# An attention and gated feed-forward kernel: the output stage's first product ordered behind the middle stage's last, the last group's chunks in another order, and their results through four buffers

## The chip, the core and the metric

The kernel runs on one core of a Trainium2 chip. The metric is the device time of one execution in microseconds (us), as the median of several runs. A profile of one execution gives the rows quoted below. TensorE (PE) does the matrix products, VectorE (DVE), ScalarE (ACT) and GpSimd (POOL) the element-wise work, and SyncE (SP) issues the transfers (DMA), one after another in a fixed order.

## What is computed

```python
# q, k, v: batch 8, heads 8, sequence 576, head size 64
scores = scale * q @ k.T + alibi_bias            # causal, window of 128
attn = softmax(scores)                           # with 1e-9 in the denominator
x = (attn @ v) as 4608 tokens x 512
gate = 1 / (1 + exp(-(x @ w_gate)))              # 512 x 1536
val = x @ w_val                                  # 512 x 1536
out = (gate * val) @ w_out                       # 1536 x 512
```

## The kernel before

All operations are first collected in a list, `Graph`. Each has an engine, a guessed cost, the keys that it reads and writes, and a wish time. `Graph.order` then plans one fixed order for every engine by these guesses, and the instructions are written in that order. At run time each engine goes through its own list in order and waits for semaphores where it depends on others. So an operation that waits holds everything behind it on its engine, and a changed key or guessed cost can move any operation.

The work has three stages. In the first, attention for 8 batches of 4 head pairs goes along with a first part of the feed-forward products (L528). The middle stage (`ffn2`, products in L662) makes gate and value for six groups of tokens, t = 0 to 5, of 768 tokens each, in halves of 384. The output stage (`last`, products in L780) multiplies the result by w_out, group after group, and writes the output.

Middle and output stage use a scheme with seven products where a plain 2 by 2 block product takes eight. An operand is first combined (sums and differences of its four blocks), then each combination is split into a high and a low part, and a product is six matmuls: two blocks times high-high, high-low and low-high. In the middle stage a chunk is one slice of 128 of the 1536 hidden columns: seven products over the combinations xc0 to xc6 (buffers ar0 to ar6), accumulated in three of the eight PSUM banks. `chunk` writes them in the order 0, 3, 4, 1, 5, 2, 6. Between them ScalarE copies partial results out (`low`, and p5 in `later_hs`), VectorE adds them to the next ones (L669), ScalarE takes a tanh (`sg`, L673) and VectorE multiplies (L677). The result of a chunk, 128 by 2 by 384, stays in a buffer `later_hs`, of which there are two, taken in turn, until a DMA has stored it in the scratch tensor `hid`.

The chunk's weights lie in one of eight slots, `w2s0` to `w2s7`, high and low part apart (w2s60 and w2s61 are slot 6). The middle stage runs groups 4 and 5 first and group 3 last. In group 3 eight chunks are left, on slots 0 to 7. When a slot's last chunk is done, the slot is filled again for the output stage: slots 0 to 5 with w_out (`wo20` to `wo25`, from the scratch `stash_o`), slots 6 and 7 with part of the hidden results of a group (`rows60` to `rows71`, from `hid`). The rest of these rows goes to `rows_xr`, where the middle stage's input was. Which rows lie where is said by

```python
    RAW = {(0, 0, 0): 0, (0, 0, 1): 1, (0, 0, 2): 2, (1, 0, 0): 3, (1, 1, 0): 4, (1, 0, 1): 5, (1, 1, 1): 6, (1, 0, 2): 7,
           (1, 1, 2): 8, (0, 1, 0): 9, (0, 1, 1): 10, (0, 1, 2): 11}
```

for (half, block, part q): places 0 to 3 are in `rows_xr`, 4 to 7 in slot 6, 8 to 11 in slot 7. The output stage goes through its combinations k in the order 0, 3, 4, 1, 5, 2, 6, each for three parts q and two output blocks j. k = 0 uses a row as it is, k = 3 a sum of two (`csum`), k = 4 this sum less a third. A combination's high and low part is a `duo`, in the buffers ar7, 0, 3, 4, 1, 5, 2, 6 in turn; all but the first are those of xc, so a duo can be written when the last middle product of that xc is done. k = 0, parts 0 to 2, are duo7, duo0 and duo3; k = 3 are duo4, duo1 and duo5; k = 4 begins with duo2 and duo6. The sum csum0 needs slot 6's rows, csum2 slot 7's.

Other buffers around the meeting of the stages: `wtmp`, two tiles in which w_out is prepared before it is stored in `stash_o`, on the tags h3 and h4; later on `csmall` and `cout0` lie there. `follow` hands a place from one set of keys to the next without an instruction.

Of the kernel before, what the change touches and what calls it, by code (L numbers as in the profile page):

```python
# [163 lines left out]
def attention_gated_ffn(ctx: ExitStack, tc: tile.TileContext, qd, kd, vd, wg, wv, wo, out):  # L164
# [334 lines left out]
    def hs(e, name="later_hs"):  # L499
        return T(moe, f"{name}{e}", [P, 2, N2] if name == "later_hs" else [P, NB], F32, tag=f"hs{e}")  # L500

# [106 lines left out]

    def ffn2(t, w, todo, F):
        made = t in held  # L610
# [39 lines left out]
        def chunk(i, fc):  # L650
            bx, by, bz = bank(), bank(), bank()
            e = turns[0] % 2
            turns[0] += 1
# [4 lines left out]
            def product(k, b, start, wk):  # L658
                def six():
                    for c in range(2):  # L660
                        for j, (xp, wp) in enumerate(((0, 0), (0, 1), (1, 0))):
                            nc.tensor.matmul(mm[b][:, 0:N2], w.tile2(i, wp)[:, wk, c * P:(c + 1) * P], combo(k, xp)[:, c],  # L662
                                             start=(start and c == 0 and j == 0), stop=(c == 1 and j == 2), skip_group_check=True)
                wa = 0 if wk < 2 else 2
                g.add("PE", 6 * (N2 / 2400 + 0.0133), six, [("ar", k, 0), ("ar", k, 1), ("w2", i, 0, wa), ("w2", i, 1, wa)],
                      [("mm", b)], 1.0e6)
# [31 lines left out]
            c, q, m = place(fc)  # L698
            move(lambda: hid[c, q, t][m].rearrange("p (h t) -> p h t", h=2), lambda: hs(e), [kp, kv], [("hid", fc, t, 0)], F, N2)

# [20 lines left out]
    def last(t):  # L721
        F = FIRST + 2
        n = 2 * N2
        for q in range(NDUO):
            for h, c in ((0, 0), (1, 0), (1, 1), (0, 1)):
                reads = [k for m in range(2) for k in g.writer if k[0] == "hid" and k[1] == 4 * q + 2 * m + c and k[2] == t]
                move(lambda h=h, c=c, q=q: raw2(h, c, q),
                     lambda h=h, c=c, q=q: hid[c, q, t][:, :, h * N2:(h + 1) * N2].rearrange("m p t -> p m t"),
                     reads, [("raw", h, c, q)], F + 0.1 * (h + c), n / 2)
        x = {(h, c, q): (lambda h=h, c=c, q=q: raw2(h, c, q)) for h, c, q in RAW}  # L730
# [22 lines left out]
        for k in ORDER:  # L753
# [19 lines left out]
            for j in range(2):  # L773
                bx, by, bz = bks[j]
                b = {0: bx, 3: bz, 4: bx, 1: by, 5: bx, 2: bz, 6: bx}[k]
                for q, (r, duo) in enumerate(ring):
                    def six(q=q, duo=duo, b=b, j=j, k=k):
                        for m in range(2):
                            for e, (xp, wp) in enumerate(((0, 0), (0, 1), (1, 0))):
                                nc.tensor.matmul(mm[b][:, 0:N2], wo2(2 * q + m, wp)[:, k, j * P:(j + 1) * P], duo(xp)[:, m],  # L780
                                                 start=(k in (0, 3, 1) and q == 0 and m == 0 and e == 0),
                                                 stop=(q == NDUO - 1 and m == 1 and e == 2), skip_group_check=True)
                    g.add("PE", 6 * (N2 / 2400 + 0.0133), six, [("ar", r, 0), ("ar", r, 1)] +
                          [("w2", 2 * q + m, p, a) for m in range(2) for p in range(2) for a in (0, 2)], [("mm", b)], 1.0e6)
                z = 4 * j
# [89 lines left out]
    for t in range(SPLIT):  # L875
        ffn2(t, w2, both + after, FIRST + 1)
    for n in range(NFC // 2):
# [7 lines left out]
    for q, k in enumerate((("wraw", 0), ("wraw", 1), "tt")):  # L885
        follow([k, ("csum", q)])
    follow([("wtmp", 0)] + [("csmall", z) for z in range(4)])
    follow([("wtmp", 1)] + [("cout", z) for z in range(4)])
    follow(["s2", "a1", "u2"] + [("cout", z) for z in range(4, 8)])
# [54 lines left out]
```

## Time and profile before

| | |
|---|---|
| runs | 1021.91, 1023.74, 1021.78 us; median 1021.91 us |
| profiled execution | 1023.78 us, of it 1022.1 us from first to last instruction (the span) |
| granted TensorE clock, mean | 0.995 |
| TensorE busy | 1001.5 us, 98% of the span |
| VectorE busy | 788.0 us, 77% |
| ScalarE busy | 536.5 us, 52% |
| GpSimd busy | 123.4 us, 12% |
| DMA | 176.82 MB, 173 GB/s in the mean |

How to read it: times in rows are from the span's start. A busy engine need not be at its peak; TensorE's granted clock (PEclk, or 1.00 and 0.50 in rows of stretches) says how much of its full clock it had. In a group's row stand line, engine, operation, output<-inputs and count, then busy time and the mean of one in ns, then the idle time before them and what ended most of it. SPq marks the issue of a transfer. In the chain of waits each row is a start, a duration and what it was.

### The profile page before, as it was taken

The numbers are of one execution on the slowest core, as the hardware profiler recorded it, in microseconds if no ns is written. First come the engines' busy times: TensorE is split into PE (matmuls) and PEld (weight loads), VectorE is DVE, ScalarE is ACT, GpSimd is POOL, SyncE is SP. The second block draws the span as 40 slices with busy tenths as digits, with TensorE's granted clock in tenths as the row PEclk, the third lists the DMA queues.
The fourth block names the chain that finished last, engine by engine and source line by source line (L and its number), as shares of the span: only waits on it lengthen the run. The fifth ranks groups of instructions, "written<-read, shape, count | busy, mean of one in ns | idle before, by whom it ended". The sixth has DMA issues, their size and how long they took to land.

```text
span 1022.1 us, 18050 instructions
## 1 busy us (share of the span) xinstructions
PE 1001.5 (98%) x6216; PEld 931.2 (91%) x6216; DVE 788.0 (77%) x2033; ACT 536.5 (52%) x1428; POOL 123.4 (12%) x217
## 2 busy tenths in 40 slices
PE   9899899999999999999999999999989999999998
PEld 7677678778888999999999999999979999999998
DVE  7999799877847997945985968757369887879783
ACT  6899879768753545534443534443234433334341
POOL 2333344323330100000000100000000000000000
PEclk9999999999999999999999999999989999999999
DMA  8777677846434543311653443527786354553601
GB/s 287 249 242 258 223 244 232 288 155 224 154 119 156 165 161 114 119 62 47 222 175 138 147 172 140 208 98 294 255 295 190 105 165 141 163 149 100 183 19 62
DMA packets 84284, 176.82 MB, mean 173 GB/s; under 512 B 7648, under 2 KB 50016, under 8 KB 84192
## 3 DMA queue, kind: packets, MB, share of 16 engines
q1 hardware_dynamic: 84192, 175.67, 51.1%
q8 instruction: 49, 0.80, 0.3%
q14 instruction: 43, 0.35, 0.1%
HBM read 117.44 MB, written 58.20 MB: 172 GB/s over the span
## 4 chain that ended last, share of the span: by engine, by line
PE 85%; DVE 6%; ACT 5%; DMA 3%; issue 1%; SPq 0%; ACTq 0%; DVEq 0%
PE mm L662 39%; PE mm L780 26%; PE mm L528 9%; PE mm L476 5%; PE mm L390 4%; PE mm L439 3%; ACT pb L414 2%; DMA qr<-in_q_dram 1%; ACT both L185 1%; DVE first L194 1%; DMA rows<-hid 1%; DMA early_xr<-xs 1%; DVE mm L403 1%; DVE xc L194 0%; DMA kr<-in_k_dram 0%
## 5 line engine op out<-in xcount | busy, mean ns | idle before, releaser
L662 PE MATMUL mm<-xc,w2s 128*128 128x384 f32 x2352 | 410.5, 334 | 1.4 <-ACT low L185 1.2
L662 PEld LDWEIGHTS mm<-xc,w2s 128*128 128x128 f32 x2352 | 407.5, 188 | 3.8 <-ACT low L185 2.6
L780 PE MATMUL mm<-duo,wo 128*128 128x384 f32 x1512 | 265.9, 336 | 4.1 <-ACT duo L185 3.3
L780 PEld LDWEIGHTS mm<-duo,wo 128*128 128x128 f32 x1512 | 264.5, 189 | 5.0 <-ACT duo L185 3.6
L528 PE MATMUL mm<-first,first 128*128 128x512 f32 x564 | 149.8, 406 | 0.6 <-DVE early_hs L547 0.3
L450 POOL TENSOR_SCALAR_AFFINE_SELECT pt<-both 128x384 f32<-128x384 f32 x192 | 105.9, 575 | 193.7 <-ACT both L185 178.4
L669 DVE TENSOR_TENSOR mm<-mm,low 128x384 f32<-128x384 f32 x112 | 62.9, 562 | 78.4 <-PE mm L662 75.2
L528 PEld LDWEIGHTS mm<-first,first 128*128 128x128 f32 x564 | 101.4, 190 | 21.3 <-issue 1.3
L673 ACT ACTIVATE sg<-mm 128x384 f32<-128x384 f32 x112 | 54.6, 491 | 112.2 <-PE mm L662 66.8
L185 ACT COPY low<-mm 128x384 f32<-128x384 f32 x112 | 53.7, 479 | 93.5 <-PE mm L662 71.6
L414 ACT ACTIVATE pb<-pb,st 128x128 f32<-128x128 f32 x216 | 84.5, 397 | 9.4 <-DVE st L411 9.3
L476 PEld LDWEIGHTS mm<-pt,vr 128*64 128x64 f32 x832 | 61.2, 137 | 12.7 <-issue 7.6
L194 DVE TENSOR_TENSOR duo<-rows,duo 128x768 fp32r<-128x768 f32 x66 | 62.8, 956 | 10.8 <-ACT duo L185 7.6
L476 PE MATMUL mm<-pt,vr 128*64 128x256 f32 (+2 forms) x832 | 67.4, 306 | 0.6 <-POOL pt L450 0.6
L185 ACT COPY both<-mm 128x384 f32<-128x384 f32 x96 | 45.6, 475 | 34.9 <-PE mm L439 22.3
L403 DVE COPY_PREDICATED mm<-early_h,mm 128x256 f32<-128x256 int32 (+1 forms) x144 | 49.2, 391 | 10.9 <-PE mm L390 10.3
L185 ACT CAST duo<-rows 128x768 fp32r<-128x768 f32 x45 | 37.1, 835 | 38.8 <-issue 19.3
L390 PE MATMUL mm<-kr,qr 64*128 64x256 f32 (+1 forms) x396 | 55.1, 381 | 0.7 <-DMA kr<-in_k_dram 0.7
L411 DVE CUSTOM_DVE_ANT_0 pb<-mm,early_h 128x128 f32<-128x128 f32 x216 | 51.5, 279 | 0.0
L390 PEld LDWEIGHTS mm<-kr,qr 64*128 64x128 f32 x396 | 38.1, 186 | 10.0 <-issue 2.2
L439 PE MATMUL mm<-ident,pb 128*128 128x128 f32 x216 | 38.5, 286 | 6.9 <-ACT both L185 5.7
L439 PEld LDWEIGHTS mm<-ident,pb 128*128 128x128 f32 x216 | 25.0, 141 | 20.9 <-ACT both L185 9.4
(117 smaller groups left out, 1119.3 us busy)
## 6 DMA issues: line engine op xcount, KB each, us to landing
hid<-later_hs SPq DMA_DIRECT2D x56, 384.0 KB, 2.3
rows<-hid SPq DMA_DIRECT2D x48, 384.0 KB, 4.1
kr<-in_k_dram SPq DMA_DIRECT2D x21, 576.0 KB, 4.7
wo<-stash_o SPq DMA_DIRECT2D x12, 896.0 KB, 6.9
vr<-in_v_dram SPq DMA_DIRECT2D x32, 288.0 KB, 3.5
xs<-xt SPq DMA_DIRECT2D x32, 288.0 KB, 2.9
stash_o<-wtmp SPq DMA_DIRECT2D x12, 768.0 KB, 3.3
rows_xr<-hid SPq DMA_DIRECT2D x24, 384.0 KB, 3.3
```

The costliest lines, as they stand in the source:

```text
L185: g.add("ACT", act_cost(n, psum), lambda: nc.scalar.copy(out(), src()), reads, writes, want, release=release, ways=[("DVE", dve_cost(n, ps ...
L194: g.add("DVE", dve_cost(n, psum, True), lambda: nc.vector.tensor_tensor(out(), a(), b(), op=ALU.subtract), reads, writes, want, port=not p ...
L390: nc.tensor.matmul(sp[bank_of(r, a)][:, a % 2, lo:], qraw(u)[rows, i // 2], kraw(u)[rows, (i - 1) * P + lo:(i + 1) * P], start=True, stop= ...
L403: g.add("DVE", dve_cost((a1 - a0) * P, psum=True), lambda b=b, a0=a0, a1=a1: nc.vector.copy_predicated(sp[b][:, a0:a1, P:], before[:, a0:a ...
L414: g.add("ACT", 0.39, lambda: nc.scalar.activation(pb()[:, e], pb()[:, e], AF.Exp, bias=st()[:, e:e + 1], scale=-1.0, accum_out=st()[:, 3 + ...
L439: nc.tensor.transpose(tp[:, e], pb()[:, e], ident)
L450: nc.gpsimd.affine_select(pt(u)[:, f0:f0 + 2 * n - 1:2, :], both(), [[0, n], step], cmp, 0.0, base=0, channel_multiplier=mult)
L476: nc.tensor.matmul(to()[e * D:(e + 1) * D, a - e * S - t0:b - e * S - t0], vraw(u)[:, c], seen, start=first, stop=last, skip_group_check=True)
L528: nc.tensor.matmul(mm[s][:, 0:wd], w.tile(kind, wi, i)[:, c * P:(c + 1) * P], xpart(x, c)[:, 0:wd], start=(k == 0 and c == 0), stop=(k == ...
L662: nc.tensor.matmul(mm[b][:, 0:N2], w.tile2(i, wp)[:, wk, c * P:(c + 1) * P], combo(k, xp)[:, c], start=(start and c == 0 and j == 0), stop ...
L669: g.add("DVE", dve_cost(N2, psum=True), lambda: nc.vector.tensor_tensor(o(), bk(b)(), a(), op=ALU.add), [("mm", b), *reads] if okeys else ...
L780: nc.tensor.matmul(mm[b][:, 0:N2], wo2(2 * q + m, wp)[:, k, j * P:(j + 1) * P], duo(xp)[:, m], start=(k in (0, 3, 1) and q == 0 and m == 0 ...
```

## The change

It has five parts. Each middle product now also reads a key `seam`, and each first product (k = 0) of the output stage's first group writes it; so these, and with them all output products behind them in the banks, are ordered behind the last middle product. The planner's guessed rate for storing `hid` and for loading rows goes from 220 to 350. The last four chunks of group 3 are taken on slots 6, 4, 5, 7 in place of 4, 5, 6, 7. The eight chunks of group 3 use four `later_hs` buffers in turn in place of two. The two new ones take the places h3 and h4, behind `wtmp` and ahead of `csmall` and `cout0`.

```diff
     def hs(e, name="later_hs"):
-        return T(moe, f"{name}{e}", [P, 2, N2] if name == "later_hs" else [P, NB], F32, tag=f"hs{e}")
+        return T(moe, f"{name}{e}", [P, 2, N2] if name == "later_hs" else [P, NB], F32, tag=f"hs{e}" if e < 2 else f"h{e + 1}")
...
-    def ffn2(t, w, todo, F):
+    def ffn2(t, w, todo, F, ends=False):
...
-            e = turns[0] % 2
+            e = turns[0] % (4 if ends else 2)
...
-                g.add("PE", 6 * (N2 / 2400 + 0.0133), six, [("ar", k, 0), ("ar", k, 1), ("w2", i, 0, wa), ("w2", i, 1, wa)],
+                g.add("PE", 6 * (N2 / 2400 + 0.0133), six, [("ar", k, 0), ("ar", k, 1), ("w2", i, 0, wa), ("w2", i, 1, wa), "seam"],
                       [("mm", b)], 1.0e6)
...
-            move(lambda: hid[c, q, t][m].rearrange("p (h t) -> p h t", h=2), lambda: hs(e), [kp, kv], [("hid", fc, t, 0)], F, N2)
+            move(lambda: hid[c, q, t][m].rearrange("p (h t) -> p h t", h=2), lambda: hs(e), [kp, kv], [("hid", fc, t, 0)], F, N2, True)
...
-                     reads, [("raw", h, c, q)], F + 0.1 * (h + c), n / 2)
+                     reads, [("raw", h, c, q)], F + 0.1 * (h + c), n / 2, True)
...
-                          [("w2", 2 * q + m, p, a) for m in range(2) for p in range(2) for a in (0, 2)], [("mm", b)], 1.0e6)
+                          [("w2", 2 * q + m, p, a) for m in range(2) for p in range(2) for a in (0, 2)],
+                          [("mm", b), *(["seam"] if t == 0 and k == 0 else [])], 1.0e6)
...
     for t in range(SPLIT):
-        ffn2(t, w2, both + after, FIRST + 1)
+        if t == SPLIT - 1:
+            for p in range(2):
+                follow([("wtmp", p)] + [("hs", 2 + p, j) for j in range(2)])
+        ffn2(t, w2, both + after if t < SPLIT - 1 else both + [after[z] for z in (2, 0, 1, 3)], FIRST + 1, t == SPLIT - 1)
...
-    follow([("wtmp", 0)] + [("csmall", z) for z in range(4)])
-    follow([("wtmp", 1)] + [("cout", z) for z in range(4)])
+    follow([("hs", 2, j) for j in range(2)] + [("csmall", z) for z in range(4)])
+    follow([("hs", 3, j) for j in range(2)] + [("cout", z) for z in range(4)])
```

What this does to the engines' lists at the meeting of the stages is shown for three of them. A name is a tile with its buffer number and an identifier: xc1 a combination of the middle stage, w2s70 the high part of slot 7, mm a PSUM bank.

TensorE before, around the first product of the output stage (L780):

```order
L662 MATMUL mm6_152<-xc1_3834,w2s70_3990 128x384
L662 MATMUL mm6_152<-xc1_3834,w2s71_4005 128x384
L662 MATMUL mm6_152<-xc1_3834,w2s70_3990 128x384 x2
L662 MATMUL mm6_152<-xc1_3834,w2s71_4005 128x384
L662 MATMUL mm6_152<-xc1_3834,w2s70_3990 128x384
L780 MATMUL mm0_146<-duo7_6839,wo200_6824 128x384
L780 MATMUL mm0_146<-duo7_6839,wo201_6827 128x384
L780 MATMUL mm0_146<-duo7_6839,wo200_6824 128x384
L780 MATMUL mm0_146<-duo7_6839,wo210_6884 128x384
L780 MATMUL mm0_146<-duo7_6839,wo211_6886 128x384
L780 MATMUL mm0_146<-duo7_6839,wo210_6884 128x384
L662 MATMUL mm1_147<-xc2_3866,w2s50_3725 128x384
```

TensorE after, at the same point:

```order
L662 MATMUL mm7_153<-xc2_3866,w2s70_3990 128x384
L662 MATMUL mm7_153<-xc2_3866,w2s71_4005 128x384
L662 MATMUL mm7_153<-xc2_3866,w2s70_3990 128x384 x2
L662 MATMUL mm7_153<-xc2_3866,w2s71_4005 128x384
L662 MATMUL mm7_153<-xc2_3866,w2s70_3990 128x384
L662 MATMUL mm5_151<-xc6_3809,w2s70_3990 128x384
L662 MATMUL mm5_151<-xc6_3809,w2s71_4005 128x384
L662 MATMUL mm5_151<-xc6_3809,w2s70_3990 128x384 x2
L662 MATMUL mm5_151<-xc6_3809,w2s71_4005 128x384
L662 MATMUL mm5_151<-xc6_3809,w2s70_3990 128x384
L780 MATMUL mm0_146<-duo7_6827,wo200_6824 128x384
L780 MATMUL mm0_146<-duo7_6827,wo201_6829 128x384
```

Before, six output products stood among the last middle products; now the last middle product (xc6 on slot 7) stands ahead of all of them.

SP before, from the load of slot 4's new weights on (wo2 for w_out, rows6 and rows7 for slots 6 and 7):

```order
L190 DMA wo240_7104<-stash_o4_108 128x1792
L190 DMA wo241_7108<-stash_o4_108 128x1792
L190 DMA hid023_125<-later_hs0_3847 128x768
L190 DMA wo250_7162<-stash_o5_109 128x1792
L190 DMA wo251_7166<-stash_o5_109 128x1792
L190 DMA hid123_143<-later_hs1_3909 128x768
L190 DMA rows60_7214<-hid010_116 128x2x384
L190 DMA rows61_7224<-hid020_122 128x2x384
L190 DMA hid023_125<-later_hs0_3847 128x768
L190 DMA rows60_7214<-hid100_128 128x2x384
L190 DMA rows61_7224<-hid110_134 128x2x384
L190 DMA rows70_7261<-hid100_128 128x2x384
```

SP after, at the same place of its list:

```order
L190 DMA rows60_7065<-hid010_116 128x2x384
L190 DMA rows61_7068<-hid020_122 128x2x384
L190 DMA hid023_125<-later_hs0_3847 128x768
L190 DMA rows60_7065<-hid100_128 128x2x384
L190 DMA rows61_7068<-hid110_134 128x2x384
L190 DMA wo240_7110<-stash_o4_108 128x1792
L190 DMA wo241_7113<-stash_o4_108 128x1792
L190 DMA hid023_125<-later_hs1_3909 128x768
L190 DMA wo250_7170<-stash_o5_109 128x1792
L190 DMA wo251_7173<-stash_o5_109 128x1792
L190 DMA hid123_143<-later_hs2_6964 128x768
L190 DMA rows70_7241<-hid100_128 128x2x384
```

The four loads into slot 6 moved from behind the loads of slots 4 and 5 to ahead of them, and the stores of `hid` come from other buffers.

VectorE before, at its last operations of the middle stage (L669 and L677) and the first sums of the output stage (L735):

```order
L669 TENSOR_TENSOR later_hs1_3909<-mm5_151,later_hs1_3909 128x384
L669 TENSOR_TENSOR mm7_153<-mm7_153,low_3748 128x384
L677 SCALAR_TENSOR_TENSOR later_hs1_3909<-sg0_852,mm7_153 128x384
L677 SCALAR_TENSOR_TENSOR later_hs1_3909<-sg1_874,later_hs1_3909 128x384
L735 TENSOR_TENSOR csum0_7269<-rows_xr_6794,rows60_7214 128x768
L735 TENSOR_TENSOR rows_xr_6794<-rows_xr_6794 128x768
L735 TENSOR_TENSOR csum1_7274<-rows60_7214,rows61_7224 128x768
L194 TENSOR_TENSOR duo4_7271<-csum0_7269,duo4_7271 128x768
```

VectorE after, from the addition for slot 5's fifth product to that for slot 7's fifth (L194 subtracts the high part, which gives the low one):

```order
L669 TENSOR_TENSOR later_hs2_6964<-mm2_148,later_hs2_6964 128x384
L735 TENSOR_TENSOR csum0_7152<-rows_xr_6794,rows60_7065 128x768
L669 TENSOR_TENSOR mm4_150<-mm4_150,low_3748 128x384
L735 TENSOR_TENSOR csum1_7161<-rows60_7065,rows61_7068 128x768
L677 SCALAR_TENSOR_TENSOR later_hs2_6964<-sg0_852,mm4_150 128x384
L677 SCALAR_TENSOR_TENSOR later_hs2_6964<-sg1_874,later_hs2_6964 128x384
L735 TENSOR_TENSOR rows_xr_6794<-rows_xr_6794 128x768
L194 TENSOR_TENSOR duo0_7183<-rows_xr_6794,duo0_7183 128x768
L735 TENSOR_TENSOR rows60_7065<-rows_xr_6794,rows60_7065 128x768
L194 TENSOR_TENSOR duo3_7195<-rows_xr_6794,duo3_7195 128x768
L669 TENSOR_TENSOR mm6_152<-mm6_152,low_3748 128x384
L669 TENSOR_TENSOR later_hs3_6996<-mm5_151,later_hs3_6996 128x384
```

Before, the output stage's sums came behind the middle stage's last multiplication; now six operations of the output stage (csum0 to duo3) stand among the middle stage's last additions, and the addition into `later_hs3`, for which the last middle product waits, comes behind them.

## Prediction

> **What bounds the kernel now.** I read the page first, for the engine that fills the span.
>
> ```profile
> span 1022.1 us, 18050 instructions
> ...
> PE 1001.5 (98%) x6216; PEld 931.2 (91%) x6216; DVE 788.0 (77%) x2033; ACT 536.5 (52%) x1428; POOL 123.4 (12%) x217
> ...
> PEclk9999999999999999999999999999989999999999
> ...
> L662 PE MATMUL mm<-xc,w2s 128*128 128x384 f32 x2352 | 410.5, 334 | 1.4 <-ACT low L185 1.2
> ...
> L780 PE MATMUL mm<-duo,wo 128*128 128x384 f32 x1512 | 265.9, 336 | 4.1 <-ACT duo L185 3.3
> ```
>
> TensorE is busy 98% of the span. The middle stage (L662) waits 1.4 us in 2352 matmuls, the output stage (L780) 4.1 us in 1512, and the one slice with a lower clock, the 31st, lies where the two meet. So I cut the meeting into stretches, TensorE alone (stretch, busy and matmuls that touch it, granted clock, DMA share, GB/s).
>
> ```profile
> 724.49:755.22 30.73, 29.86 (x168) 1.00 0.79 264
> 755.22:760.65 5.43, 1.28 (x5) 0.83 0.99 330
> 760.65:765.18 4.53, 4.53 (x14) 0.50 0.61 197
> 765.18:1018.70 253.52, 253.51 (x1461) 1.00 0.43 130
> ```
>
> The last row gives the dense rate, 253.52 / 1461 = 0.1735 us a matmul, 1.04 us for a product of six. In the first, 168 matmuls need 29.15 us, so 1.58 us are lost. 36 of them are output matmuls, the six products ordered early; 1476 remain, 1461 of them in the last row. The 15 others took 9.96 us in the middle rows where 2.60 would do: 7.36 us lost, part idle, part at clock 0.50. Together 8.94 us. The chain of waits tells why.
>
> ```profile
> 750.27 0.57 DVE later_hs L677
> ...
> 750.85 0.33 SPq L190
> ...
> 751.24 5.64 DMA rows<-hid
> ...
> 756.90 0.97 DVE csum L735
> ...
> 758.77 0.95 DVE csum L735
> 759.72 0.88 DVE duo L194
> ...
> 760.65 258.05 PE mm L780 x1474
> ```
>
> The rows of slot 6 stand on SP behind a result's store that waits for VectorE; they land 6 us later; then csum and its split, and only then TensorE. After 760.65 nothing else is on the chain but TensorE, to the last 3 us. TensorE's own waits from 700 to 800 us agree:
>
> ```profile
> PE mm L780 <- ACT duo L185: 3.3, 1, 3.3
> PE mm L780 <- DVE duo L194: 0.9, 1, 0.9
> PE mm L662 <- ACT low L185: 0.7, 2, 0.6
> ```
>
> One idle of 3.3 us is followed by half clock; the waits of up to 0.6 us are not. The Trainium skill, "TensorE: Matmul & The Clock Gate", section "Why this matters for your kernels", states that an idle of about 3 us returns the array to half clock; the trace agrees here.
>
> **The change, part by part.** Matmuls, copies and bytes stay; only order and places change.
>
> *Seam and chunk order.* All six early products go behind the middle stage, so its end E comes sooner: 132 matmuls after 724.49, 22.9 us, E = 747.4 if dense. From there 1512 x 0.1735 = 262.4 us. In the order of after, consecutive products into one bank have a whole product of another bank between them (1.04 us), and the copy or addition between takes 0.48 to 0.57 us (the two ScalarE and VectorE rows at the end of this part's fences), so I take the waits of 1.58 us as gone, down to slot 7's chunk. Slot 6's chunk now ends 19 products before E (727.6), slot 4's 14 (732.8), slot 5's 7 (740.1), slot 7's at E.
>
> *Transfers.* Each slot's end releases loads on SP, which go one after another. Sizes, SP's issues, DMA by stretch, and the landing of wo:
>
> ```profile
> hid<-later_hs SPq DMA_DIRECT2D x56, 384.0 KB, 2.3
> rows<-hid SPq DMA_DIRECT2D x48, 384.0 KB, 4.1
> ...
> wo<-stash_o SPq DMA_DIRECT2D x12, 896.0 KB, 6.9
> ```
> ```profile
> 715.15 0.80 SPq L190 DMA_DIRECT2D wo<-stash_o  x2
> ...
> 749.68 0.88 SPq L190 DMA_DIRECT2D rows<-hid  x2
> ...
> 751.24 5.16 SPq L190 DMA_DIRECT2D rows<-hid  x4
> ```
> ```profile
> 728.00:736.00 8.00, 1.00 0.80 277
> 736.00:744.00 8.00, 1.00 0.94 296
> 744.00:752.00 8.00, 1.00 0.86 297
> 752.00:760.00 8.00, 0.93 1.01 341
> ```
> ```profile
> 701.00:709.00 8.00, 1.00 1.03 386
> ```
> ```profile
> DMA to landing us min/median/max: 4.6/6.9/9.9
> ```
>
> Divided by their shares the four stretches give 346, 315, 345 and 338 GB/s, and 701 to 709, with stores among the loads, 375. I take 340, the middle of the reading stretches, and 2 us from issue to landing beside the bytes (the shortest wo, 4.6 us, less 0.92 MB at 340). Slot 2's chunk ends 27 products before E, at 719.3 (wo22 was issued at 715.15 before, since that chunk ended earlier). From then to wo25 there are 8 wo, 4 rows and 4 stores, 10.49 MB or 30.9 us: wo25 lands at 752.2. One store and slot 7's four rows make 12.45 MB: the last row at 757.9. At 315 they land at 754.6 and 760.8; at 375 at 749.3 and 754.5. The Trainium skill, "DMA: Bandwidth & Descriptors", section "Specifications", gives a core about 358 GB/s of HBM. By that wo25 would land, as an estimate, at 750.6 and the sum lose its 0.5 us for late rows below; the 386 measured above passes the figure, the reading stretches stay under it.
>
> *Who needs them.* In after wo25 is used first in the fifth output product (E + 4.7), csum2 by the 14th (E + 13.5). From the last row to csum2's split VectorE has csum2, two other splits and the split, 0.95 + 3 x 0.87 = 3.6 us: 761.5.
>
> *VectorE ahead of E.* Ahead of the addition into later_hs3 that the last middle product waits for, VectorE now has six wide operations of the output stage (csum0 to duo3). Their pace, and the narrow ones:
>
> ```profile
> 757.90 0.96 DVE L735 TENSOR_TENSOR rows_xr<-rows_xr 128x768 f32<-128x768 f32 x1
> 758.77 0.95 DVE L735 TENSOR_TENSOR csum<-rows,rows 128x768 f32<-128x768 f32 x1
> 759.64 0.95 DVE L194 TENSOR_TENSOR duo<-csum,duo 128x768 fp32r<-128x768 f32 x1
> ```
> ```profile
> L669 DVE TENSOR_TENSOR mm<-mm,low 128x384 f32<-128x384 f32 x112 | 62.9, 562 | 78.4 <-PE mm L662 75.2
> ...
> L185 ACT COPY low<-mm 128x384 f32<-128x384 f32 x112 | 53.7, 479 | 93.5 <-PE mm L662 71.6
> ```
>
> They start 0.87 us apart: 6 x 0.87 + 5 x 0.55 = 8.0 us. The queue is free for csum0 at about E - 8.6 = 738.8, after the addition for slot 5's fifth product (it ends 9 products before E; 0.2 us of hand-over and 0.55). csum0 needs slot 6's third row: 6.03 MB after 719.3, 17.7 us at 340 and the 2 us, 739.0; the fourth at 740.2. So VectorE is through at 746.8 to 748.2, and the last middle product, due at E - 1.04 = 746.4, is 0.4 to 1.8 us late. I take 1.0: E' = 748.4. Then wo25 (752.2) is in time for 753.1, and csum2's split (761.5) for 761.9; at 315 GB/s they are 1.5 and 2.5 us late, the second holding the first. Between 0 and 2.5 I take 0.5, near the 340 end.
>
> *Four buffers.* later_hs2 and 3 take wtmp's places, so the copy into later_hs2 waits for wtmp's store.
>
> ```profile
> L190 SPq DMA_DIRECT2D stash_o<-wtmp x12: 319/319/320, 504.0 to 706.7; - x12
> ...
> DMA to landing us min/median/max: 3.2/3.3/10.6
> ```
>
> Issued by 706.7, the slowest landing gives 717.3 for wtmp1; wtmp0 goes 0.79 MB ahead, 2.1 us at 375, about 715.2. The copy into later_hs2 is due at 714.5 and TensorE asks for it at 717.0; later_hs3 is due near 720. Hidden, with 1.8 us to spare; if the store lands with wtmp1's, 0.8 us late. The moved wtmp0 split on ScalarE (1536 wide) stands where a copy is due two products later; at most some 0.8 us too. I take 0 for both.
>
> *The planner's faster prices* for stores and rows move a few products and splits further ahead (from the later groups on). They stay inside a dense stretch; their bound is what all L662 waits cost, 1.4 us either way, and I take 0.
>
> *Sum.* Profiled execution 1023.78 - 8.94 + 1.0 + 0.5 = 1016.3. It stands 1.87 over the median of 1021.91; the runs fall in two groups, 1021.8 to 1021.9 and 1023.7 to 1023.8, and no row says where the 1.87 lies. If in the stall or its clock, it goes with it (1016.3); if elsewhere, the median becomes 1014.5. Nothing decides, so I take the middle, 1015.4. The clock gate page, Part 1, says that the gate works in free-running windows of 3.41 us; by that, as an estimate, a run's half-clock stretch may be a window shorter, 1.7 us of time, and the sum would be 1016.3.
>
> **How it can go otherwise.** The likeliest case spans 1013.4 (no late row, VectorE's 0.4, the 1.87 elsewhere) to 1018.6 (VectorE's 1.8, rows 2 us late, the 1.87 in the stall).
>
> Rival one: the transfers bind. At 315 GB/s csum2's split comes 2.5 us late, with VectorE's 1.8 this is 1019.1; if the idle reaches the 3.3 us of the row above, half clock follows, 3.2 us lost for a stretch like that of before (0.83 over 5.43 us is 1.85 us at 0.50, and 4.53 us more). 1019.1 to 1022.3, or 1.87 less where that lies elsewhere. For it speaks the DMA share near 1.0; against it, that most loads are issued 5 to 8 us sooner than before.
>
> Rival two: the stall only moves. If csum1 or duo0 still came at 758 to 760, TensorE would idle ahead of them, now with no middle product to fill: 1021 to 1023. Against it: their rows are released at 727.6 instead of 749.7.
>
> Rival three, slower: csum0 on VectorE holds the middle stage. Each microsecond that slot 6's rows land after 739 stops the last products one for one, since output products may not pass; over 3.3 us idle adds 1.7 to 3.4 of clock. Landing at 746 gives back 7 + 2.5: 1024. It decides from a landing of about 745; slot 6's rows would need 16 us where the page has 4.1.
>
> **How the numbers follow.** Likeliest case 0.77, rival one 0.13, two 0.06, three 0.04. The range 1013.3 to 1018.8 takes the likeliest case and the near end of rival one, some 8 in 10. About 0.2% (2.0 us) is what this measurement can tell from no change: below 1019.9 lie the first case and most of rival one, 0.87; within it the rest of that and rival two, 0.09; slower, rival three, 0.04.
>
> **What would show it.** Right: no L780 matmul before the last L662; that last one near 748; no clock below 1.00 at the seam; csum0 starting 738.5 to 740 on VectorE; output stage 262 to 264 us. Wrong: an idle of TensorE over 2 us after 747, wo25 landing after 754, or a wait of later_hs2's copy on a stash store.

## Result, and the profile after

The changed kernel takes 1014.74 us in the median (1013.91 to 1015.70, 4 runs), the kernel before 1021.85 us beside it (1021.61 to 1023.74, 4 runs). The ratio is 0.9927, its 95% interval 0.9910 to 0.9944: faster by 5.7 to 9.2 us. The profiled execution took 1015.13 us, 8.65 us less than that of before.

The page after, in the rows that answer to those shown of before:

```profile
span 1013.4 us, 18087 instructions
...
PE 997.5 (98%) x6216; PEld 927.8 (92%) x6216; DVE 784.1 (77%) x2025; ACT 544.6 (54%) x1435; POOL 125.1 (12%) x218
...
PEclk9999999999999999999999999999999999999999
...
L662 PE MATMUL mm<-xc,w2s 128*128 128x384 f32 x2352 | 410.2, 335 | 1.0 <-ACT low L185 0.9
...
L780 PE MATMUL mm<-duo,wo 128*128 128x384 f32 x1512 | 262.2, 334 | 0.0
```

The output stage's 4.1 us of waits are gone, the middle stage's went from 1.4 to 1.0, and no slice has a lower clock. TensorE's timeline from 700 to 800 us (start, duration, what) has two rows, and there is no wait in it:

```profile
699.82 48.13 PE L662 MATMUL mm<-xc,w2s 128*128 128x384 f32 x272
747.80 52.51 PE L780 MATMUL mm<-duo,wo 128*128 128x384 f32 x302
```

Cut at the meeting of the stages (stretch, busy, matmuls, granted clock, DMA share, GB/s):

```profile
699.82:747.80 47.98, 47.91 (x274) 1.00 0.93 359
747.80:1010.10 262.30, 262.24 (x1513) 1.00 0.43 135
```

The output stage begins at 747.8 and takes 262.3 us, which is the dense rate. The last middle row ends at 699.82 + 48.13 = 747.95 (ends are modelled and overlap the next start a little); in before's timeline it is this one, which ends at 755.49, 7.5 us later:

```profile
753.14 2.35 PE L662 MATMUL mm<-xc,w2s 128*128 128x384 f32 x12
```

What VectorE does in after around that end (timeline):

```profile
738.97 0.95 DVE L735 TENSOR_TENSOR csum<-rows_xr,rows 128x768 f32<-128x768 f32 x1
...
746.04 0.55 DVE L669 TENSOR_TENSOR later_hs<-mm,later_hs 128x384 f32<-128x384 f32 x1
...
756.64 0.95 DVE L735 TENSOR_TENSOR csum<-rows,rows 128x768 f32<-128x768 f32 x1
...
759.31 0.95 DVE L194 TENSOR_TENSOR duo<-csum,duo 128x768 fp32r<-128x768 f32 x1
```

csum0 starts at 738.97, the addition for which the last middle product waits ends at 746.6, and csum2's split is through at 760.3.

The yardstick for all kernels is TensorE from 700 to 780 us. The row of before, and then that of after:

```profile
700.00:780.00 80.00, 74.98 (x410) 0.96 0.79 273
```
```profile
700.00:780.00 80.00, 79.93 (x458) 1.00 0.83 305
```

After has 48 matmuls more in the same 80 us; at 0.1735 us each that is 8.3 us, nearly the whole gain of 8.65. By 700 us the two executions had done 2082 and 2080 matmuls of the middle stage, so what was won was won here.

### The profile page after: what moved, and what is told of

Its sections match the earlier page's. It is cut to its first block, busy times and chain, and to the rows that moved or that the text cites. A ratio compares the mean times of both kernels' runs of the same rounds, so it can differ in the third digit from the quotient of the medians.

```text
span 1013.4 us, 18087 instructions
## 1 busy us (share of the span) xinstructions
PE 997.5 (98%) x6216; PEld 927.8 (92%) x6216; DVE 784.1 (77%) x2025; ACT 544.6 (54%) x1435; POOL 125.1 (12%) x218
## 4 chain that ended last, share of the span: by engine, by line
PE 83%; DVE 8%; ACT 5%; DMA 2%; issue 1%; SPq 0%; ACTq 0%; DVEq 0%
PE mm L662 38%; PE mm L780 26%; PE mm L528 8%; PE mm L476 4%; PE mm L390 4%; PE mm L439 2%; ACT pb L414 2%; ACT both L185 1%; DVE first L194 1%; ACT pb L434 1%; DVE mm L403 1%; DMA wraw<-in_moe_w_gate_dram 1%; DVE w2s L194 1%; DVE pb L411 1%; DMA early_xr<-xs 1%
## 5 line engine op out<-in xcount | busy, mean ns | idle before, releaser
L780 PE MATMUL mm<-duo,wo 128*128 128x384 f32 x1512 | 262.2, 334 | 0.0
L780 PEld LDWEIGHTS mm<-duo,wo 128*128 128x128 f32 x1512 | 262.1, 188 | 0.0
L669 DVE TENSOR_TENSOR mm<-mm,low 128x384 f32<-128x384 f32 x112 | 63.0, 564 | 70.0 <-PE mm L662 66.4
L194 DVE TENSOR_TENSOR duo<-rows,duo 128x768 fp32r<-128x768 f32 x66 | 62.9, 957 | 10.6 <-ACT duo L185 8.6
L185 ACT CAST duo<-rows 128x768 fp32r<-128x768 f32 x48 | 40.0, 837 | 54.1 <-PE mm L780 29.5
```

Of the source, the lines that this page charges most:

```text
L185: g.add("ACT", act_cost(n, psum), lambda: nc.scalar.copy(out(), src()), reads, writes, want, release=release, ways=[("DVE", dve_cost(n, ps ...
L194: g.add("DVE", dve_cost(n, psum, True), lambda: nc.vector.tensor_tensor(out(), a(), b(), op=ALU.subtract), reads, writes, want, port=not p ...
L669: g.add("DVE", dve_cost(N2, psum=True), lambda: nc.vector.tensor_tensor(o(), bk(b)(), a(), op=ALU.add), [("mm", b), *reads] if okeys else ...
```

## The experiments

The change has parts that can be taken one by one. Four theories were told apart. Rows theory (the prediction's): the chunk order brings slot 6's rows early, and that closes the stall. Seam theory: ordering the output products behind the middle stage does it. Buffer theory: stores of results land late behind the loads, and four buffers make that harmless. The fourth, added later ("third theory" in the expectations), is that the planner's prices decide, since they set how many output products stand early. A reserve theory followed from the first results: the output products that are ready are a reserve, which must last from the middle stage's end until the late rows have become operands. All times are medians; before was 1022.46 (15 runs) beside the first four kernels, 1022.47 (15) beside the next four, 1022.64 (23) beside the last four; after itself was measured beside 1021.85 (4). In the diffs, which are cut short, the comments are added. "Early" counts the output products ahead of the last middle one in the trace, "end" is the end of the last middle row (one execution each, and these begin the middle stage anywhere from 336.4 to 338.0 us), and the last column is the yardstick, the matmuls from 700 to 780 us: a kernel with one less has lost 0.17 us more there.

| kernel | time | ratio to before, 95% | early | end | matmuls |
|---|---|---|---|---|---|
| after | 1014.74 | 0.9910 to 0.9944 | 0 | 747.9 | 458 |
| before | 1022.5 | | 6 | 755.5 | 410 |
| seam alone | 1022.35 | 0.9993 to 1.0010 | 0 | 754.3 | 412 |
| order alone | 1021.05 | 0.9973 to 0.9991 | 6 | 756.1 | 427 |
| prices alone | 1016.52 | 0.9926 to 0.9953 | 2 | 750.2 | 447 |
| stores' price alone | 1020.00 | 0.9966 to 0.9983 | 4 | 750.9 | 429 |
| four buffers alone | 1016.26 | 0.9925 to 0.9950 | 0 | 746.4 | 449 |
| seam and four buffers | 1017.03 | 0.9933 to 0.9957 | 0 | 746.0 | 441 |
| after less seam | 1014.64 | 0.9914 to 0.9938 | 1 | 748.7 | 460 |
| after less order | 1014.49 | 0.9915 to 0.9942 | 0 | 746.4 | 459 |
| after less two buffers | 1015.00 | 0.9917 to 0.9942 | 2 | 749.0 | 461 |
| after less prices | 1015.67 | 0.9916 to 0.9941 | 0 | 746.6 | 452 |
| after, six products early | 1014.76 | 0.9916 to 0.9940 | 6 | 753.0 | 457 |
| before, filled stall | 1020.72 | 0.9972 to 0.9989 | 6 | 754.7 | 437, 18 of them added |

### The seam alone

```diff
 (before)
-... ("w2", i, 0, wa), ("w2", i, 1, wa)],            # middle product reads
+... ("w2", i, 0, wa), ("w2", i, 1, wa), "seam"],
-[("mm", b)], 1.0e6)                                 # output product writes
+[("mm", b), *(["seam"] if t == 0 and k == 0 else [])], 1.0e6)
```

> The kernel before with the seam alone (old rates, old chunk order, two buffers). Rows theory (the gain is that slot 6's rows are released before the other loads): the middle stage ends near 748, slot 6 ends only three products before that, its rows are issued near 744 and 746, land near 752, and csum0 starts near 752; the first six output products last to 754, so TensorE still waits 1 to 2.5 us for duo4, at full clock: 1016 to 1018.5. Seam theory (the gain is that no output product is spent before the wait): 1014 to 1015.5, as the changed kernel. Buffer theory: little gain, 1020 to 1022.

Measured: 1022.35 us, ratio 1.0002 [0.9993, 1.0010]: nothing. TensorE's timeline at the meeting:

```profile
744.41 2.36 PE L662 MATMUL mm<-xc,w2s 128*128 128x384 f32 x12 [1.67 <-ACT later_hs L185]
...
750.59 3.70 PE L662 MATMUL mm<-xc,w2s 128*128 128x384 f32 x12 [2.32 <-ACT later_hs L185]
754.09 11.31 PE L780 MATMUL mm<-duo,wo 128*128 128x384 f32 x62
```

ScalarE's copies into `later_hs` that it waits for:

```profile
743.88 0.48 ACT L185 COPY later_hs<-mm 128x384 f32<-128x384 f32 x1 [2.42 <-DMA hid<-later_hs]
...
750.06 0.48 ACT L185 COPY later_hs<-mm 128x384 f32<-128x384 f32 x1 [2.31 <-DMA hid<-later_hs]
```

The output stage no longer stalls behind the middle stage's end; the idle has moved ahead of it. A copy must wait until the buffer's last store has landed, the bank is not read, and the next product into that bank waits. Before, output products stood in these places and filled them. The half clock behind the second idle is seen in the 12 matmuls that took 3.70 us. So the seam theory falls. The rows theory's figure for this kernel missed; the buffer theory's little gain held, though 1022.35 lies 0.35 us over its range.

### One part taken out of after

Without the seam, without the chunk order, and with two buffers:

```diff
 (after, three kernels)
-("w2", i, 1, wa), "seam"],                             # 1: seam taken out on both sides
+("w2", i, 1, wa)],
...
-both + [after[z] for z in (2, 0, 1, 3)]                # 2: old chunk order
+both + after
...
-            e = turns[0] % (4 if ends else 2)          # 3: two buffers
+            e = turns[0] % 2
```

> The changed kernel without the seam. One output product then stands ahead of the last middle product, no more. Rows theory and buffer theory: as the changed kernel, 1013.5 to 1016, with slot 6's rows issued near 728. Seam theory: most of the gain lost, 1018 to 1022.

> The changed kernel with the last four chunks on slots 4, 5, 6, 7 again. Slot 6 ends 7 products before the end of the middle stage, near 740; its rows are issued near 740 and 742 behind wo25. Rows theory in its strict form: csum0 late, a wait of TensorE of 2 us or more behind the first six output products, 1016.5 to 1019. By the queue of transfers worked out with 340 GB/s the rows land near 750 and csum0's split near 753, just in time for 753.6: 1014 to 1016. Seam and buffer theory: as the changed kernel, 1013.5 to 1016.

> The changed kernel with two result buffers. Slot 5's and slot 7's chunks then copy into buffers whose stores were issued 6 to 8 us before, behind other transfers. Buffer theory: the copies wait 2 us or more for the stores and TensorE with them, 1017 to 1020. Rows and seam theory: within 1 us of the changed kernel, 1013.7 to 1016.

Measured: 1014.64, 1014.49 and 1015.00 us; none differs from after by what can be told. The kernel without the chunk order is the instructive one. Its slot 6 rows are asked for at 739.2 to 741 in place of 728 to 730, csum0 comes 9 us later than in after, and TensorE does not wait (two timelines):

```profile
747.91 0.96 DVE L735 TENSOR_TENSOR csum<-rows_xr,rows 128x768 f32<-128x768 f32 x1 [0.32 <-DMA rows<-hid]
```
```profile
746.25 28.95 PE L780 MATMUL mm<-duo,wo 128*128 128x384 f32 x164
```

Behind 746.4 stand six products of k = 0, whose rows lie in `rows_xr` already: 6.2 us in which csum0 can still become an operand. So early rows are not needed where these six are still to be done. With two buffers ScalarE's copies again wait for stores (3.3 us in three waits), but products of the other stage cover it, and TensorE waits 0.2 us.

### One part alone, and the prices taken out

```diff
 (before, three kernels)
-            e = turns[0] % 2                            # buffers alone
+            e = turns[0] % (4 if ends else 2)
...
-both + after                                            # order alone
+both + [after[z] for z in (2, 0, 1, 3)]
...
-[("hid", fc, t, 0)], F, N2)                             # prices alone: stores
+[("hid", fc, t, 0)], F, N2, True)
-[("raw", h, c, q)], F + 0.1 * (h + c), n / 2)           # and rows
+[("raw", h, c, q)], F + 0.1 * (h + c), n / 2, True)
```

The fourth kernel is after with the old prices in these two lines.

> The kernel before with the four result buffers alone: no seam, the old chunk order, the old prices. In its lists no output product stands ahead of the last middle product, and slot 6's rows are asked for some seven products before the middle stage's end. Buffer theory (what is lost at the meeting comes from stores of results that land 8 to 11 us after their issue behind the loads, while only two buffers take the results; four cure it): 1014 to 1016.5, no wait of ScalarE's copy into later_hs for a store, clock 1.00 at the meeting. Rows theory (slot 6's rows must be asked for well ahead, by the chunk order): they come late again, an idle of 2 us or more ahead of a csum1, csum2 or duo product, 1018 to 1022.

> The kernel before with the chunk order 6, 4, 5, 7 alone: two buffers, no seam, the old prices; output products stand among the last middle products again. Rows theory: slot 6's rows come early, the sums are ready, 1014 to 1016.5. Buffer theory: the copies into later_hs wait 1.6 to 2.4 us for stores as in the kernel with the seam alone, and as the waits move to another product an idle of 2 to 3 us with half clock behind it stays: 1018 to 1022.

> The kernel before with the planner's faster prices for stores and rows alone: two buffers, the old chunk order, no seam; slot 6's rows stand behind slot 5's load on SP as before. Rows theory and buffer theory both: little is gained, 1019 to 1023, since neither the rows nor the buffers come sooner. A third theory, that the planner's list is what counts (its guess of 220 GB/s made it order output products ahead of middle ones too early and leave the sums too late): 1014 to 1017, without an idle over 1 us at the meeting.

> The changed kernel with the old prices: seam, chunk order and four buffers. Rows theory and buffer theory: 1014 to 1016, as the changed kernel. Third theory (the planner's prices count): 1017 to 1021, with an idle of more than 1 us at the meeting.

Measured: buffers alone 1016.26, order alone 1021.05, prices alone 1016.52, after with the old prices 1015.67. Two single parts, buffers and prices, each bring 6 of the 8 us; the order alone, on which the prediction's story rested, brings 0.9 to 2.8. TensorE's timeline with four buffers alone, and with the faster prices alone:

```profile
734.67 11.77 PE L662 MATMUL mm<-xc,w2s 128*128 128x384 f32 x67
746.29 6.40 PE L780 MATMUL mm<-duo,wo 128*128 128x384 f32 x36
753.99 0.61 PE L780 MATMUL mm<-duo,wo 128*128 128x384 f32 x2 [1.30 <-ACT duo L185]
754.99 20.24 PE L780 MATMUL mm<-duo,wo 128*128 128x384 f32 x114 [0.38 <-DVE duo L194]
```
```profile
747.84 2.37 PE L662 MATMUL mm<-xc,w2s 128*128 128x384 f32 x12 [1.56 <-ACT later_hs L185]
750.06 4.67 PE L780 MATMUL mm<-duo,wo 128*128 128x384 f32 x26
754.99 20.34 PE L780 MATMUL mm<-duo,wo 128*128 128x384 f32 x114 [0.26 <-DVE duo L194]
```

With four buffers no copy waits for a store, the planner puts no output product early, and the middle stage ends dense at 746.4. The six products of k = 0 (36 matmuls) then run, and what is left is an idle of 1.30 and 0.38 us ahead of csum0's product. Slot 6's rows come late, but just in time: csum0 starts at 750.69, and in before its product could begin 1.88 us after its start, which would be 752.57 here, when the six products are just ending (746.45 + 6.24 = 752.69). What TensorE waits for is ScalarE's list (timeline, four buffers alone):

```profile
752.73 0.49 ACT L743 ACTIVATE csmall<-mm 128x384 f32<-128x384 f32 x1 [0.55 <-PE mm L780]
753.12 1.56 ACT L185 CAST duo<-csum 128x768 fp32r<-128x768 f32 x2
```

The cast that makes csum0's high part stands behind a copy (`csmall`) that itself waits for the last of the six products, so it begins 1.5 us after csum0 is through (751.65). The kernel with the seam and four buffers, below, shows the same (copy at 752.30, cast at 752.69). A kernel with the cast first was not tried. With the prices alone the planner believes that stores land sooner and puts two products early in place of six; one wait for a store, 1.56 us, is left, and 0.26 ahead of the output product. For the prices alone the rows and the buffer theory, 1019 to 1023, both missed; the third theory's time held, not its "no idle over 1 us". For the buffers alone the buffer theory's 1014 to 1016.5 held. For after with the old prices it is the other way round: the third theory's 1017 to 1021 missed, though the idle of over 1 us that it named came (1.12 us).

Order alone: csum0 comes at 743.6, 13 us sooner than before, and the stall shows up elsewhere:

```profile
756.67 14.83 PE L780 MATMUL mm<-duo,wo 128*128 128x384 f32 x84 [0.58 <-ACT sg L673]
772.99 0.61 PE L780 MATMUL mm<-duo,wo 128*128 128x384 f32 x2 [1.48 <-ACT duo L185]
774.50 5.71 PE L780 MATMUL mm<-duo,wo 128*128 128x384 f32 x30 [0.90 <-DVE duo L194]
```

```profile
770.83 0.95 DVE L735 TENSOR_TENSOR csum<-rows,rows 128x768 f32<-128x768 f32 x1
```

The waits of 1.48 and 0.90 us are for csum2's product: csum2 stands late on VectorE (second block), 14.7 us behind the stage's end, where after has 8.7. This is the prediction's second rival, the stall that only moves, at 1021 to 1023 us; it is real for the order alone. But a late csum2 is not enough for it: in after with the old prices it comes 16.7 us behind the stage's end (at 746.56), and TensorE does not wait for it there.

```profile
763.28 0.95 DVE L735 TENSOR_TENSOR csum<-rows,rows 128x768 f32<-128x768 f32 x1
```

That kernel has the same chunk order but no product early, so six more products were left to run. The buffer theory's time for this kernel held, its reason did not: the copies into `later_hs` waited 0.3 us for a store in all. Beside the order none of the other three parts is needed to mend it, as the kernels with one of them taken out show; whether one alone is enough was not tried.

### Seam and buffers, and the stores' price

```diff
 (before: seam and four buffers, edits as above)
 (before: stores' price alone)
-[("hid", fc, t, 0)], F, N2)
+[("hid", fc, t, 0)], F, N2, True)
```

> The kernel before with the seam and the four buffers, old chunk order and prices: it differs from the kernel with the seam alone (1022.35) only in the buffers. Buffer theory: the two waits of the middle stage for stores (4.0 us) and the half clock behind them go, 1014.5 to 1017. If the seam itself were what costs there, or the late rows of slot 6 were: 1019 to 1022.5.

> The kernel before with the faster price for the stores of hid alone, rows at the old one. In its list four output products stand ahead of the last middle product, where before has six, the one with both prices two. Reserve theory: between the two, 1017.5 to 1021. If only the price of the rows counts: 1021 to 1023.

Measured: 1017.03 us, 0.03 over the buffer theory's range, and 1020.00 us, inside the reserve theory's. The buffers take the seam from nothing to 4.4 to 6.9 us gained: they were what held it up. The stores' price alone falls between, with four products early. Its timeline:

```profile
750.70 2.25 PE L780 MATMUL mm<-duo,wo 128*128 128x384 f32 x12
755.35 0.62 PE L780 MATMUL mm<-duo,wo 128*128 128x384 f32 x2 [2.41 <-ACT duo L185]
757.21 17.96 PE L780 MATMUL mm<-duo,wo 128*128 128x384 f32 x93 [1.24 <-DVE duo L194]
```

Here csum0 starts at 753.47, and its product can begin 1.88 us later. Two products were left after the middle stage's end at 750.86: 750.86 + 2.08 + 2.41 = 755.35. In before csum0 started at 756.90, the product could begin at 758.78, none was left at 755.49, and the idle was 3.29. So the idle behind the middle stage is the time at which csum0's first half (the high part) is an operand, less the stage's end, less 1.04 us for each ready product that was not taken early. It is the reserve that differs most: csum0 starts 1.4 us behind the stage's end in before, 2.6 with the stores' price, 1.0 with both prices and 4.2 with four buffers, and the products left at the end are none, two, four and six.

### Six products early in the changed kernel

```diff
 (after, without the seam; order of the list only)
+    for z, o in enumerate(firsts[:12]):                 # first 12 output products
+        a, b = (o, mids[-1]) if z in (0, 1, 3, 4, 6, 7) else (mids[-1], o)
+        a.outs.append(b.seq)                            # a ahead of b; mids[-1]: last middle product
+        b.left += 1
     g.play()
```

> The changed kernel with four buffers, order and prices as they are, but six output products (duo7, duo0, duo4 and duo1, whose rows and weights are there) placed by hand ahead of the last middle product, the others behind it. Reserve theory (products that need nothing from slot 7 are a reserve that must last from the middle stage's end until slot 7's rows have become operands; a product taken early is missing there, and the end comes 1.04 us later for each): middle stage ends near 754, duo0 and csum2's split 14 to 18 us later at 764 to 766 where TensorE asks from 762 on, an idle of 1.5 to 4.5 us, with half clock behind it where it is over 2 us: 1016.5 to 1021. Buffer theory alone (only the buffers count, early products cost nothing): 1014 to 1016.

Measured: 1014.76 us, ratio 0.9928 [0.9916, 0.9940]. The reserve theory in its strong form is refuted: six products early cost nothing here. Timeline:

```profile
752.81 16.46 PE L781 MATMUL mm<-duo,wo 128*128 128x384 f32 x92
769.45 5.84 PE L781 MATMUL mm<-duo,wo 128*128 128x384 f32 x32 [0.18 <-DVE duo L194]
```

The middle stage ends 5.0 us later than in after, and slot 7's rows are asked for 5.0 us later. But csum0 (737.93) and all that follows from slot 6's rows are long done, so fifteen more products are ready behind the end (92 matmuls), and TensorE waits 0.2 us for a split. An early product costs only if the next one is not ready. In before both held: the six were spent, and slot 6's rows were late.

### The stall of before, filled with other matmuls

```diff
 (before; order of the lists unchanged)
+if t == 0 and k == 3 and q == j == m == e == 0:
+    for _ in range(18):                                 # overwritten by the product behind them
+        nc.tensor.matmul(mm[b][:, 0:N2], wo2(0, 0)[:, 0, 0:P], duo3[:, 0, 0], start=True, stop=False, ...)
```

> The kernel before with 18 added matmuls (3.1 us, the same tile each time, overwritten by the product behind them) ahead of the product of duo4 that waits 3.3 us; all other lists stay. If the clock comes down because TensorE idles, the clock stays at 1.00 there while the wait stays as long, and the share of the half clock is gained: 2.1 us for 14 matmuls and 0.6 for two, 1019 to 1020.5. If the clock falls for another reason, or the dummies delay what is waited for: 1022 to 1024.

Measured: 1020.72 us, ratio 0.9981 [0.9972, 0.9989], 1.1 to 2.9 us faster by doing 18 matmuls more; the median is 0.2 us over the range expected. Timeline, and the clock in the stretch of the stall:

```profile
754.56 3.29 PE L782 MATMUL mm<-duo,wo 128*128 128x384 f32 x18
758.49 0.62 PE L784 MATMUL mm<-duo,wo 128*128 128x384 f32 x2 [0.65 <-ACT duo L185]
760.36 14.85 PE L784 MATMUL mm<-duo,wo 128*128 128x384 f32 x83 [1.25 <-DVE duo L194]
```
```profile
754.00:766.00 12.00, 10.11 (x56) 1.00 0.84 281
```

The clock stays at 1.00, where before's mean in this stretch is 0.72. The high and the low part of csum0's split come 1.87 us apart in both kernels (758.78 and 760.65 before), so what the two matmuls between them gain in speed is waited for again: 0.4 us of the expectation. So of the 7 to 8 us between before and after some 2 are half clock, as a consequence of the idle, and the rest is mostly idle.

## Why the prediction was right, and where its reasons were not

The sum held: 1016.3 for the profiled execution, 1015.13 measured; 1015.4 for the median, 1014.74 measured.

- *The 8.94 us lost at the meeting*: right. From the point where 133 middle matmuls are left (724.14 us in before, 724.54 in after) to the start of the last output matmul (1018.35 and 1009.70) before takes 294.2 us and after 285.2, 9.0 us less.
- *The middle stage's end*, 748.4: measured 747.8. VectorE's delay was taken as 1.0 of 0.4 to 1.8; the last middle product's weights waited 0.21 us for the addition into `later_hs`. That is 0.8 less; after came 0.4 us later to the 133 matmuls, and 0.2 lies in where the stretch was cut, so 0.6 us of difference is seen. The order of the six operations and csum0's start (739.0 against 738.97) were right.
- *Late rows*, 0.5: measured 0, csum2's split was through at 760.3 in place of 761.5. The transfers went faster than the 340 GB/s taken (the stretches from 728 on, in the changed kernel):

```profile
728.00:736.00 8.00, 1.00 1.02 407
736.00:744.00 8.00, 1.00 1.03 415
744.00:752.00 8.00, 1.00 0.91 335
```

- *The output stage*, 262.4: measured 262.3. With the two above that is 1016.3 - 0.6 - 0.5 - 0.1 = 1015.1, the profiled execution to 0.1 us.
- *The 1.87 us* of the profiled execution over the median, half taken off: in 23 further runs before's median was 1022.64, 1.1 us under that execution, and after's profiled execution stands 0.4 over its median. Most of before's excess lay outside the stall. The first rows of the middle stage, in before and then in after:

```profile
337.90 6.71 PE L662 MATMUL mm<-xc,w2s 128*128 128x384 f32 x36
```
```profile
336.73 6.70 PE L662 MATMUL mm<-xc,w2s 128*128 128x384 f32 x36
```

This execution of before came to the stage 1.17 us later; its clock was 0.50 from 52.2 to 55.7 us, where after has 1.00. Of the fourteen executions profiled three had this early stretch and began the stage at 337.6 to 338.0 us, the other eleven at 336.4 to 337.1. By the prediction's own rule ("elsewhere") the median would then have been near 1014.5.
- *wtmp's store and the copy into later_hs2*, 0: right.

```profile
715.07 0.48 ACT L185 COPY later_hs<-mm 128x384 f32<-128x384 f32 x1 [0.44 <-DMA stash_o<-wtmp]
```

- *Seam and chunk order* as what closes the stall: this step failed as a cause. The prediction gave them the whole 8.94 us and took buffers and prices at 0. Alone, the seam measured 0 (-1.0 to 0.7 us) and the order 0.9 to 2.8; buffers and prices, alone, 6.2 (5.1 to 7.7) and 6.0 (4.8 to 7.6). By the medians each is worth at most about a microsecond in the presence of the others, so the sum could be right with the shares wrong. What was overlooked is one wait, ScalarE's copy into `later_hs` for a store, 1.8 us in two waits in the trace of before, of which this is the longer:

```profile
744.87 0.48 ACT L185 COPY later_hs<-mm 128x384 f32<-128x384 f32 x1 [1.60 <-DMA hid<-later_hs]
```

It cost TensorE nothing there because output products stood in its place, and these were then missing as cover for slot 6's late rows. It is the planner that put them there: six with its guess of 220 for a store, four with 350, two with 350 for the rows too, none with four buffers. That it did so because it expected the copy to wait fits these counts; the plan itself was not looked into. The guess was not wrong in kind; from 700 to 765 us these stores of before landed late (count, size, median us to landing), against 2.3 us over the whole run:

```profile
hid<-later_hs SPq DMA_DIRECT2D x8, 384.0 KB, 7.9
```

- *"In the order of after ... I take the waits of 1.58 us as gone"*: true of after, but only with the buffers or the prices; in the kernel with the seam alone the waits in this place were 4.8 us.
- *Rivals*: transfers did not bind. The stall that only moves did not come in after, but in the order alone. csum0 on VectorE held the middle stage of after by 0.2 us.

Shown by the runs: there are two places where TensorE can run dry, the copies that wait for stores ahead of the middle stage's end, and csum0's operand behind it. Before filled the first by emptying the second. Four buffers close the first and leave 1.7 us at the second, by ScalarE's list; the prices leave 1.6 and 0.3; the order closes the second at csum0 and leaves another at csum2; the seam closes the second and opens the first. The kernels with two or three of buffers, prices and order close both to within 1.3 us; all but the one with all three had the seam too, so two of the three without the seam were not tried. No kernel tried beats the changed one by what can be told.

## What to carry to other kernels

When work of the next stage stands among the last of a stage, ask which wait it fills; forbidding it without removing that wait only moves the idle. Behind the stage's end the idle is the time of the first late operand, less the end, less the ready work not yet spent, so there are three ways to close it, and they do not add up. Look, too, at what stands ahead of that operand in its own engine's list. Where a planner sets the order by guessed prices, the guess is a lever: here both prices together brought as much as the buffers (6.0 and 6.2 us), the stores' price alone 2.6.

## What the runs showed of the hardware

A shorter idle than expected can bring half clock. With the seam and four buffers TensorE idled 1.30 and 0.37 us between 752 and 755 us, with the buffers alone 1.30 and 0.38 at the same place. Behind it the first ran at half clock for 3.41 us, a loss of 1.7 us, and the second did not. What differs is where the idle lies on a grid: in every trace with a half-clock stretch, its start and end lie a whole number of steps of 3.413 us apart from each other and from the change of the clock after the last matmul. TensorE by steps of this grid, first the one kernel, then the other:

```profile
751.91:755.32 3.41, 1.74 (x9) 1.00 0.77 294
755.32:758.74 3.42, 3.42 (x13) 0.50 0.12 12
758.74:762.15 3.41, 3.41 (x21) 1.00 0.62 227
```
```profile
749.48:752.89 3.41, 3.21 (x19) 1.00 1.05 396
752.89:756.30 3.41, 1.93 (x9) 1.00 0.60 224
756.30:759.72 3.42, 3.42 (x21) 1.00 0.28 62
```

In the first both idles lie in one step, 1.67 us together; in the second a step ends between them, and they make 0.20 and 1.48. Over all steps at full clock in the fourteen traces, seven were followed by a step at half clock. TensorE had idled 1.62, 1.67, 1.67, 1.72, 2.32, 2.52 and 3.29 us in them; the longest idle in a step without it was 1.64, the next 1.56 (the ends of matmuls are modelled, so the last hundredths are uncertain). So in these traces the sum of the idle in a step counts, and not the length of one gap: a single gap of 1.67 us (seam alone, 1.64 of it in one step) did not bring half clock, and 1.30 and 0.37 did. The 1.48 and 0.90 us of the order alone did not bring half clock; they make 0.86 and 1.52 in two steps. How a kernel's idle falls on the grid can differ from one execution to the next: with the buffers alone four executions at a mean clock of 1.000 took 1016.06 to 1016.32 us, and the fifth, at 0.998, took 1017.96; which step it lost was not traced.

The Trainium skill, "TensorE: Matmul & The Clock Gate", section "Why this matters for your kernels", asks to avoid gaps over about 3 us; the first row block shows a loss at 1.30 and 0.37. "Part 1" of the same page of the Trainium skill has windows of 3.41 us that run freely, and the grid of the traces agrees with that.

The queue moved 407 and 415 GB/s in stretches of 8 us with stores among the loads, and 335 behind them. The prediction quoted 358 GB/s from the Trainium skill, "DMA: Bandwidth & Descriptors", section "Specifications". Another page of the Trainium skill, "Perfetto Trace Analysis", section "Roofline", says that a core alone can pull more than that share, up to the 435 of its 16 engines, and the trace agrees with it.
